# Linear attention followed by a mixture of adapters: where the gating steps stand in a hand-written order, how the last three outputs are grouped, and which queue stores the last one

## The chip, the cores and the metric

The kernel runs on one core of a Trainium2 chip. The metric is the device time of one execution in microseconds (us). Three runs of the kernel before took 119.56, 119.78 and 119.87 us; the median is 119.78. The core has a matrix engine (TensorE, "PE" in the profile, its weight loads "PEld"), a vector engine (VectorE, "DVE"), a scalar engine (ScalarE, "ACT"), GpSimd ("POOL") and a queue that only issues transfers here (SyncE, "SP"). Each engine executes its own instructions in the order in which they were written; engines wait for each other through semaphores.

## The reference

Inputs q, k and v have the shape (8 batches, 8 heads, 576 positions, 64). First comes a linear attention with cosine and sine weights on the positions, then, on its output x (4608 rows of 512), a mixture of 8 adapters of rank 16, of which each row uses its best two:

```python
q_p, k_p = phi(q, cos, sin), phi(k, cos, sin)   # relu, times cos and times sin: 128 features
kv  = einsum('bhsf,bhsd->bhfd', k_p, v);  z = sum(k_p, axis=2)
x   = einsum('bhsf,bhfd->bhsd', q_p, kv) / (einsum('bhsf,bhf->bhs', q_p, z) + 1e-6)
logits = x @ w_gate                              # 8 experts, the top 2 of each row
w      = softmax over the two chosen logits
out    = x + sum over the two of  w[e] * (x @ A[e]) @ B[e]
```

With two chosen logits l1 and l2 the softmax is a sigmoid: the weight of a chosen expert is sigmoid(2*l - (l1 + l2)), and that is how the kernel computes it.

## The kernel before

The output is made in 36 tiles of 128 rows and 512 columns; one step of the main loop ("slot" n, from 0 to 35) makes one tile of x. The work on one tile n goes through these functions:

- `transp_q(n)`, PE, L192: 16 small matmuls turn q and multiply it by the cos and sin diagonals, into two buffers of the two-buffer PSUM pool `qd`. `evac_q`, ACT, L208: two copies with relu. `move_q` is both; slot n calls it for tile n+1.
- `numden(n)`, PE, L226 and L231: numerator and denominator of the attention for all 8 heads, into the single PSUM tile `nd`.
- `normalise(n)`, DVE, L238 and L240: reciprocal and product, giving the tile `xt`. As there is one `nd`, `numden(n+1)` can only start when `normalise(n)` is through, and `normalise(n+1)` needs `numden(n+1)`.
- `transp_x(n)`, PE, L248, and `evac_x(n)`, DVE, L254: x transposed through the PSUM tile `xz`, giving `xT`. `evac_x(n)` is called at the start of slot n+1.
- `logits(n)`, PE, L274: four matmuls of 144 columns give x times all adapters A and x times the gate, into the single PSUM tile `za`.
- The gating of a group of three tiles: `gate_a` on DVE (L283 to L291: top values, their sum, mask, argument), `gate_sig` on ACT (L300, the sigmoid, written into `za` as well), `gate_b` on DVE (L307 and L309: the weights `em` and the weighted `zg`; after it `za` is free for the next group).
- `transp_z`, PE, L322: `zg` transposed into the second half of `xz`. The next `evac_x` takes it along (896 instead of 512 columns); the tile's tail is then `zgT`. Such a slot is in the table `move_at`.
- `delta(n)`, PE, L338 and L339: the identity times x, plus `zgT` times B, into one of two PSUM tiles `cd`, or, in slots in which `cd` holds a kv sum, into a `qd` buffer. `evac_o`, ACT, L347: copy to `osb`. `store`, L357 and L360: one transfer of 256 KB (two of 128 KB for a tile that mixes two batches), issued by SP.

In between the loop makes the kv sums of the next batches: `kv` on PE (L176, four or five columns of eight matmuls per slot, in 14 of the slots), whose scaled k comes from POOL (L152), ACT (L147) and DVE (L149, L161). All q, k and v have buffers of their own, and POOL issues their loads (L58) far ahead.

The order is written out by hand: the calls inside `with tc.manual_schedule()` are each engine's order. Tables tell in which slot something happens: `kv_at`, `relu_at`, `pool_at`, `logits_at`, `gate_a_at`, `gate_b_at`, `move_at`. In the kernel before, tiles 0 to 32 form eleven groups (0 to 10) of three, then come a group of two (33, 34) and a group of one (35). In a slot n the order is: `evac_x(n-1)`, `normalise(n)`, `move_q(n+1)`, `gate_sig` of a group whose slot for `gate_b` this is, the kv work, the due deltas with their copies and stores, `transp_x(n)`, `transp_z`, `gate_b`, k scaling, then `logits` ahead of `numden(n+1)`, or behind it in a slot with a `gate_b`, and last `gate_a`. What is left after slot 35 (a delta of group 9, all of group 10 but its gating, and the groups 11 and 12) follows behind the loop, the two last groups interleaved.

Of the kernel before, what the change touches and what calls it, by code (L numbers as in the profile page):

```python
# [8 lines left out]
FP32 = mybir.dt.float32  # L9
# [10 lines left out]
def kernel(ctx, tc, q, k, v, w_gate, A, Bw, out):  # L20
# [14 lines left out]
    p_kp = ctx.enter_context(tc.tile_pool(name="p_kp", bufs=3))  # L35
    p_qpt = ctx.enter_context(tc.tile_pool(name="p_qpt", bufs=6))
    p_kv = ctx.enter_context(tc.tile_pool(name="p_kv", bufs=3))
    p_x = ctx.enter_context(tc.tile_pool(name="p_x", bufs=12))
    p_xt = ctx.enter_context(tc.tile_pool(name="p_xt", bufs=6))
    p_g = ctx.enter_context(tc.tile_pool(name="p_g", bufs=3))  # L40
    p_o = ctx.enter_context(tc.tile_pool(name="p_o", bufs=8))
    qd = ctx.enter_context(tc.tile_pool(name="qd", bufs=2, space=bass.MemoryType.PSUM))
# [212 lines left out]
        if g is not None:  # L255
            zgT_t[g] = t[:, DCH:]

    groups = [list(range(i, min(i + 3, NT - 3))) for i in range(0, NT - 3, 3)]
    groups += [[NT - 3, NT - 2], [NT - 1]]
    group_of = {n: g for g, t in enumerate(groups) for n in t}  # L260

    def logits(n):
        g = group_of[n]
        i = n - groups[g][0]
        if i == 0:
            if g == len(groups) - 2:
                t = qd.tile([128, 512], FP32, name="zb", tag="qd")
            else:
                t = ps.tile([128, 512], FP32, name="za")
            za_t[g] = t[:, 0:3 * ZW].rearrange("p (i z) -> p i z", z=ZW)  # L270
            u_t[g] = t[:, 3 * ZW:3 * ZW + 3 * E].rearrange("p (i e) -> p i e", e=E)
        xT = xT_t.pop(n)
        for c in range(DCH):
            nc.tensor.matmul(out=za_t[g][:, i, :], lhsT=xT[:, c, :], rhs=AW[:, :, c, :],  # L274
                             start=(c == 0 and i == 0), stop=(c == DCH - 1),
                             skip_group_check=True)
# [19 lines left out]
    def gate_sig(g):  # L296
        n = len(groups[g])
        t, mask = g_t[g]
        u = u_t.pop(g)
        nc.scalar.activation(u[:, 0:n], t[:, 0:n], AF.Sigmoid)  # L300
        g_t[g] = (u, mask)
# [11 lines left out]

    def zT_ps(g):
        n = len(groups[g])
        at = 512 + (256 if g == len(groups) - 1 else 0)
        return xz[:, at:at + n * 128].rearrange("p (c s) -> p c s", c=n)

    def transp_z(g):
        zg = g_t.pop(g)  # L320
        for i in range(len(groups[g])):
            nc.tensor.transpose(out=zT_ps(g)[:, i], in_=zg[:, i], identity=ident)  # L322

    def evac_z(g):
        n = len(groups[g])
        zgT_t[g] = t = p_g.tile([128, 3, 128], BF16, name="zgT")
        nc.vector.tensor_copy(t[:, 0:n], zT_ps(g))

    dx_n = [0]

    def delta(n, own=True):
        g = group_of[n]
        if own:
            dx = cd[dx_n[0] % 2]
            dx_n[0] += 1
        else:
            dx = qd.tile([128, DM], FP32, name="dx", tag="qd")
        nc.tensor.matmul(out=dx, lhsT=ident, rhs=xt_t.pop(n), start=True, stop=False)  # L338
        nc.tensor.matmul(out=dx, lhsT=zgT_t[g][:, n - groups[g][0], :], rhs=Ball,  # L339
                         start=False, stop=True)  # L340
        osb_t[n] = dx

    def evac_o(n, eng="act"):
        src = osb_t[n]
        osb_t[n] = t = p_o.tile([128, DM], FP32, name="osb")
        if eng == "act":
            nc.scalar.copy(t, src)  # L347
        else:
            nc.vector.tensor_copy(t, src)

    def store(n):
        t = osb_t.pop(n)
        (b, s), (b1, s1) = tokens(n)
        if mixed(n):
            for rows_, b in ((lo, b), (hi, b1)):
                dst = out[b * S:(b + 1) * S, :].rearrange("(r s) d -> s r d", s=NS)[s]
                nc.sync.dma_start(out=dst, in_=t[rows_, :])  # L357
        else:
            dst = out[b * S:(b + 1) * S, :].rearrange("(r s) d -> r s d", s=NS)[:, s:s + 2, :]
            nc.sync.dma_start(out=dst, in_=t)  # L360


    kv_at, relu_at, pool_at, act_at, dve_at = {}, {}, {}, {}, {}
# [1 line left out]
    def put(at, step, what):  # L365
        at.setdefault(step, []).append(what)
# [18 lines left out]
                put(kv_at, first - ahead, (b, s))  # L385


    logits_at, gate_a_at, gate_b_at, move_at = {}, {}, {}, {}
    free = 5
    for g, t in enumerate(groups[:-2]):  # L390
        at = [max(n + 1, t[-1], free) for n in t]
        for n, a in zip(t, at):
            put(logits_at, a, n)
        free = at[-1] + (1 if g == len(groups) - 3 else 2)
        put(gate_a_at, free - 1, g)
        put(gate_b_at, free, g)
        put(move_at, free + 1, g)
    put(logits_at, NT - 2, NT - 3)

    def gate(g):  # L400
        gate_a(g)
        gate_sig(g)

    with tc.manual_schedule():
        for s in range(6):
            make_diag(s)
        wu = qd.tile([128, DM], FP32, name="wu", tag="qd")
        for i in range(24):
            nc.tensor.matmul(out=wu, lhsT=ones, rhs=wide, start=True, stop=True)  # L409
        for s in range(NS):  # L410
            scale_k(0, s, ("act" if s < 7 else "dve", "dve"))
            kv(0, s)
        nc.scalar.activation(warm, halfpi, AF.Sigmoid)
        for s in range(6, NS):
            make_diag(s)
        load_k(1)
        load_v(1)
        load_q(1)
        load_k(2)
        load_weights()  # L420
        load_v(2)
        load_q(2)
        load_k(3)
        load_v(3)
        load_k(4)
        load_q(3)
        load_v(4)
        kv_out(0)
        transp_q(0)
        evac_q(0, 0, "dve")  # L430
        evac_q(0, 1)
        numden(0)

        g10, g11, g12 = range(len(groups) - 3, len(groups))
        todo = []
        for n in range(NT):
            end = n == NT - 1
            if n > 0:
                g = move_at.get(n - 1, (None,))[0]
                evac_x(n - 1, g)  # L440
                if g is not None:
                    todo += groups[g]
            normalise(n)
            if not end and n != 3:
                move_q(n + 1)
            for g in gate_b_at.get(n, ()):
                gate_sig(g)
            for b, s in kv_at.get(n, ()):
                kv(b, s)
                if kv_n[b] == NS:  # L450
                    kv_out(b)
            if n == 3:
                move_q(n + 1)
            if end:
                transp_z(g10)
                logits(NT - 2)
            now = todo[:2 if len(todo) > 3 else 1]
            del todo[:len(now)]
            for d in now:
                delta(d, n not in kv_at)  # L460
                evac_o(d)
                store(d)
            transp_x(n)
            for g in move_at.get(n, ()):
                if not end:
                    transp_z(g)
            for g in gate_b_at.get(n, ()):
                gate_b(g)
            for b, s, i in dve_at.get(n, ()):
                scale_k1(b, s, i, "dve")  # L470
            for b, s0, s1 in relu_at.get(n, ()):
                relu_k(b, s0, s1)
            for b, s in pool_at.get(n, ()):
                scale_k(b, s)
                if s == 6:
                    if b + 3 < B:
                        load_k(b + 3)
                    if b + 2 < B:
                        load_q(b + 2)
                    if b + 3 < B:  # L480
                        load_v(b + 3)
            if n not in gate_b_at:
                for t in logits_at.get(n, ()):
                    logits(t)
            if n + 1 < NT:
                numden(n + 1)
            if n in gate_b_at:
                for t in logits_at.get(n, ()):
                    logits(t)
            for g in gate_a_at.get(n, ()):  # L490
                gate_a(g)
            for b, s, i in act_at.get(n, ()):
                scale_k1(b, s, i, "act")


        def finish(d, eng="act"):
            delta(d)
            evac_o(d, eng)
            store(d)

        evac_z(g10)
        evac_x(NT - 1)
        for d in todo + groups[g10][:1]:
            finish(d)
        logits(NT - 1)
        gate(g11)
        finish(NT - 5)
        gate(g12)
        gate_b(g11)
        transp_z(g11)  # L510
        finish(NT - 4)
        gate_b(g12)
        evac_z(g11)
        transp_z(g12)
        finish(NT - 3)
        evac_z(g12)
        finish(NT - 1, "dve")
        finish(NT - 2)

# [1 line left out]
_INS = ['q', 'k', 'v', 'moe_w_gate', 'moe_A', 'moe_B']  # L521
_OUTS = [((4608, 512), 'float32')]
# [25 lines left out]
```

## Time and profile before

| | |
|---|---|
| median of three runs | 119.78 us (119.56 to 119.87) |
| the profiled execution | 120.3 us, of it a span of 118.5 us from the first to the last instruction |
| mean granted TensorE clock | 0.997 |
| PE busy | 99.0 us, 84% of the span |
| DVE busy | 81.8 us, 69% |
| ACT busy | 76.8 us, 65% |
| POOL busy | 59.1 us, 50% |
| read from and written to memory | 28.85 MB and 9.44 MB |

Times in the views are counted from the start of the span, so the profiled execution's own time is 1.8 us more than its span. A matmul's end is modelled, and a busy PE is not a PE at its peak. The view of stretches gives, for one stretch of time, its length and each engine's busy time in it, then the granted clock, the share of the 16 DMA engines that was busy (values over 1 are a full set of engines) and GB/s. The view of waits gives who waited for whom, the sum, how often, and the longest. The chain that ended last is a list of start, length and what.

### The profile page before, as it was taken

To read this page: it belongs to the slowest core of one execution; us is meant where nothing else is said; L and a number is where in the kernel's file an instruction comes from. 1 tells how busy PE (TensorE), PEld (TensorE's weight loads), DVE (VectorE), ACT (ScalarE), POOL (GpSimd) and SP (SyncE) were. 2 spreads that over 40 slices of the span, in tenths; PEclk is the share of its full clock that TensorE was granted. 3 is DMA by queue.
4 is the path that set the end of the run, shared out by engine and by line. 5 is a ranking of instruction groups with operands and counts; after the bars stand their busy time and mean duration, and the time that the engine had idled before them with its cause. 6 is when DMAs were issued, how large, how long until landed. Compare 5 with 4: busy or idle time off the path is not lost.

```text
span 118.5 us, 4729 instructions
## 1 busy us (share of the span) xinstructions
PE 99.0 (84%) x1946; PEld 75.6 (64%) x1964; DVE 81.8 (69%) x293; ACT 76.8 (65%) x167; POOL 59.1 (50%) x118
## 2 busy tenths in 40 slices
PE   2997687868997999979999969989999999769720
PEld 1337567657885878758877857668787886656200
DVE  5697599389769765879667764797568637688620
ACT  5088579676357586688669835867779558574720
POOL 5982222278999994999990039719900000000000
PEclk9999999999999999999999999999999999999998
DMA  3999999999999999999999999999973333322892
GB/s 46 379 207 207 210 208 207 188 205 208 208 208 208 212 243 249 266 257 259 268 248 248 257 264 248 216 255 260 250 213 112 114 68 128 143 88 88 306 317 88
DMA packets 19654, 24.75 MB, mean 209 GB/s; under 512 B 2609, under 2 KB 14513, under 8 KB 19633
## 3 DMA queue, kind: packets, MB, share of 16 engines
q0 software_dynamic: 13856, 13.84, 69.9%
q1 hardware_dynamic: 5776, 10.62, 26.7%
q8 instruction: 15, 0.25, 0.8%
q14 instruction: 7, 0.05, 0.1%
HBM read 28.85 MB, written 9.44 MB: 323 GB/s over the span
## 4 chain that ended last, share of the span: by engine, by line
PE 36%; DMA 34%; DVE 9%; POOL 9%; ACT 4%; issue 4%; POOLq 0%; ACTq 0%
DMA q<-in_q_dram 23%; DMA v<-in_v_dram 12%; PE cd L176 8%; PE qd L192 7%; POOL kp L152 5%; PE xz L248 5%; PE za L274 5%; PE nd L231 4%; DVE xt L240 3%; PE cd L338 2%; DVE zg L309 2%; ACT qpT L208 2%; PE cd L339 2%; PE xz L322 1%; PE dx L338 1%
## 5 line engine op out<-in xcount | busy, mean ns | idle before, releaser
L208 ACT ACTIVATE qpT<-qd 128x512 bf16<-128x512 f32 x71 | 38.6, 595 | 23.5 <-PE qd L192 23.2
L254 DVE COPY xT<-xz 128x512 bf16<-128x512 bf16 (+1 forms) x36 | 17.1, 475 | 14.1 <-PE xz L322 8.8
L152 POOL TENSOR_SCALAR kp<-k,cos_tab 128x256 bf16<-128x256 bf16 x42 | 19.8, 471 | 13.1 <-DVE k L161 12.6
L240 DVE TENSOR_TENSOR xt<-nd,rden 128x512 bf16<-128x512 f32 x36 | 24.9, 692 | 1.2
L192 PE MATMUL qd<-diag,q 128*64 128x128 bf16 x576 | 23.0, 222 | 1.6 <-DMA q<-in_q_dram 1.6
L192 PEld LDWEIGHTS <-q 128*64 128x64 bf16 x576 | 17.2, 109 | 4.3 <-DMA q<-in_q_dram 2.0
L152 POOL TENSOR_SCALAR kp<-k,sin_tab 128x256 bf16<-128x256 bf16 x42 | 19.8, 470 | 0.0
L176 PE MATMUL cd<-v,kp 64*128 64x128 bf16 x576 | 19.0, 217 | 0.9 <-DMA v<-in_v_dram 0.7
L248 PEld LDWEIGHTS <-xt 128*128 128x128 bf16 x144 | 10.6, 115 | 12.5 <-DVE xt L240 8.3
L231 PE MATMUL nd<-kvsb,qpT 128*128 128x65 bf16 (+1 forms) x320 | 17.6, 195 | 0.9 <-DVE qpT L210 0.5
L176 PEld LDWEIGHTS <-kp 64*128 64x128 bf16 x576 | 16.3, 94 | 2.7 <-issue 1.0
L248 PE MATMUL xz<-ident,xt 128*128 128x128 bf16 x144 | 14.4, 223 | 4.1 <-DVE xt L240 3.5
L347 ACT COPY osb<-cd 128x512 f32<-128x512 f32 x24 | 14.1, 593 | 3.5 <-PE cd L339 3.4
L231 PEld LDWEIGHTS <-qpT 128*128 128x128 bf16 (+1 forms) x320 | 12.8, 99 | 2.1 <-DVE qpT L210 0.5
L274 PE MATMUL za<-AW,xT 128*128 128x144 bf16 x136 | 11.7, 225 | 2.1 <-DVE zg L309 2.1
L226 PE MATMUL nd<-eps_hi,ones 128*128 128x4 bf16 x72 | 11.6, 169 | 0.0
L274 PEld LDWEIGHTS <-xT 128*128 128x128 bf16 x144 | 9.7, 97 | 2.8 <-issue 2.4
L58 POOL DMA_DIRECT2D v<-in_v_dram x8 | 6.7, 839 | 5.1 <-DMA q<-in_q_dram 4.3
L238 DVE RECIPROCAL rden<-nd 128x8 f32<-128x8 f32 x36 | 7.3, 202 | 2.1 <-PE nd L231 2.0
L409 PE MATMUL wu<-wide,ones 128*128 128x512 bf16 x24 | 6.8, 449 | 2.2 <-DVE AW L111 2.2
L347 ACT COPY osb<-dx 128x512 f32<-128x512 f32 x11 | 6.4, 592 | 2.8 <-remote 2.8
L339 PE MATMUL cd<-Ball,xT 128*128 128x512 bf16 x18 | 6.8, 380 | 1.5 <-DVE xT L254 0.8
(66 smaller groups left out, 122.0 us busy)
## 6 DMA issues: line engine op xcount, KB each, us to landing
out_dram<-osb SPq DMA_DIRECT2D x32, 256.0 KB, 5.9
v<-in_v_dram POOLq DMA_DIRECT2D x8, 576.0 KB, 18.8
q<-in_q_dram POOLq DMA_DIRECT2D x8, 576.0 KB, 19.9
k<-in_k_dram POOLq DMA_DIRECT2D x7, 576.0 KB, 18.1
k0f<-in_k_dram SPq DMA_DIRECT2D x1, 1152.0 KB, 5.5
out_dram<-osb SPq DMA_DIRECT2D x8, 128.0 KB, 3.8
AW<-in_moe_A_dram POOLq DMA_DIRECT2D x1, 128.0 KB, 18.2
Ball<-in_moe_B_dram POOLq DMA_DIRECT2D x1, 128.0 KB, 16.5
```

Source lines behind the costliest of these rows:

```text
L152: nc.gpsimd.tensor_scalar(out=dst, in0=src, scalar1=tab, scalar2=1.0, op0=ALU.mult, op1=ALU.mult)
L176: nc.tensor.matmul(out=kvz[par][:, g], lhsT=kp_t[b][pr, s, g], rhs=v_rhs(b, g, s, pr), start=(first and g == 0), stop=(last and g == G - 1))
L192: nc.tensor.matmul(out=t[cols, j, 2 * gi:2 * gi + 2, :], lhsT=q_b[b][:, 2 * gp + gi, s, :], rhs=diag[:, s, i], start=(j == 0 and gi == 0), ...
L208: nc.scalar.activation(t, src, AF.Relu)
L226: nc.tensor.matmul(out=nd[:, gg, D:4 * W:W], lhsT=ones, rhs=eps_hi, start=True, stop=False, skip_group_check=True)
L231: nc.tensor.matmul(out=nd[pr, gg, j * W:(j + 1) * W], lhsT=qpT[:, j, pr], rhs=kv_t[b][:, h % 2, h // 2, :], start=False, stop=(j == 3), sk ...
L240: nc.vector.tensor_tensor(out=xt, in0=nd[:, :, :, 0:D], in1=rden.rearrange("p (g j) -> p g j", g=2).to_broadcast([128, 2, 4, D]), op=ALU.mult)
L248: nc.tensor.transpose(out=xz[:, c * 128:(c + 1) * 128], in_=x[:, c], identity=ident)
L254: nc.vector.tensor_copy(t[:, 0:c], xz[:, 0:c * 128].rearrange("p (c s) -> p c s", c=c))
L274: nc.tensor.matmul(out=za_t[g][:, i, :], lhsT=xT[:, c, :], rhs=AW[:, :, c, :], start=(c == 0 and i == 0), stop=(c == DCH - 1), skip_group_ ...
L339: nc.tensor.matmul(out=dx, lhsT=zgT_t[g][:, n - groups[g][0], :], rhs=Ball, start=False, stop=True)
L347: nc.scalar.copy(t, src)
```

## The change

Six things are changed.

1. The groups: twelve groups of three, so tiles 33, 34 and 35 are one group (11).
2. The tables for logits and gating. All logits of a group are now either `late` (behind `transp_x`, always ahead of `numden(n+1)`) or `early` (directly behind `transp_q`); up to group 7 all three tiles' logits stand in one slot, from group 8 on the third is `early` in the next one. `gate_a` stands in slot `at`, `gate_b` in `at + 1`, `move_at` is `at + 2`.
3. The order in a slot: `gate_a` and `gate_b` stand directly behind `normalise` on DVE, `gate_sig` stands in the slot of its `gate_a`, behind the copies of the deltas on ACT. `gate_b` so comes a slot after its sigmoid.
4. The loop ends at slot 34; slot 35 and what follows is written out. `zgT` of group 10 is copied by ACT, that of group 11 in two parts by DVE and ACT.
5. In the last group the products of x with the identity (`delta_x`) come ahead of the transposed `zg`, the products with B (`delta_z`) behind it; DVE copies the output of tile 34, ACT those of 33 and 35; the store of tile 35 is issued by ACT's queue.
6. The pool of `xt` has 14 buffers instead of 12, that of `xT` 7 instead of 6.

The slots that result, from 20 on (before | after):

```
slot  logits before    gate_a/gate_b/move   delta  | logits after         gate_a/gate_b/move   delta
20    18,19 (kv)       - / 5 / -            13     | -            (kv)    - / 5 / -            13
21    20    (kv)       - / - / 5            14     | 18,19,20     (kv)    - / - / 5            14
22    -                6 / - / -            15     | -                    6 / - / -            15
23    21,22            - / 6 / -            16     | -                    - / 6 / -            16
24    23               - / - / 6            17     | 21,22,23             - / - / 6            17
25    -     (kv)       7 / - / -            18     | -            (kv)    7 / - / -            18
26    24,25 (kv)       - / 7 / -            19     | 24,25        (kv)    - / 7 / -            19
27    26               - / - / 7            20     | 26 early             8 / - / 7            20
28    -                8 / - / -            21     | -                    - / 8 / -            21
29    27,28 (kv)       - / 8 / -            22     | 27,28        (kv)    - / - / 8            22
30    29    (kv)       - / - / 8            23     | 29 early     (kv)    9 / - / -            23,24
31    -                9 / - / -            24     | -                    - / 9 / -            25
32    30,31            - / 9 / -            25     | 30,31                - / - / 9            26
33    32               10 / - / 9           26     | 32 early             10 / - / -           27
34    33               - / 10 / -           27     | 33                   - / 10 / -           28
```

The core of the diff:

```diff
-    groups = [list(range(i, min(i + 3, NT - 3))) for i in range(0, NT - 3, 3)]
-    groups += [[NT - 3, NT - 2], [NT - 1]]
+    groups = [list(range(i, i + 3)) for i in range(0, NT, 3)]
...
-    def evac_z(g):
-        n = len(groups[g])
+    def evac_z(g, parts):
         zgT_t[g] = t = p_g.tile([128, 3, 128], BF16, name="zgT")
-        nc.vector.tensor_copy(t[:, 0:n], zT_ps(g))
+        for eng, i, j in parts:
+            if eng == "act":
+                nc.scalar.copy(t[:, i:j], zT_ps(g)[:, i:j])
+            else:
+                nc.vector.tensor_copy(t[:, i:j], zT_ps(g)[:, i:j])
...
-    free = 5
-    for g, t in enumerate(groups[:-2]):
-        at = [max(n + 1, t[-1], free) for n in t]
-        for n, a in zip(t, at):
-            put(logits_at, a, n)
-        free = at[-1] + (1 if g == len(groups) - 3 else 2)
-        put(gate_a_at, free - 1, g)
-        put(gate_b_at, free, g)
-        put(move_at, free + 1, g)
-    put(logits_at, NT - 2, NT - 3)
+    prev = 5
+    for g, t in enumerate(groups[:-1]):
+        tight = g > 7
+        at = max(t[-1] + (1 if tight else 2), prev + 1)
+        if g == 1:
+            at += 1
+        for n in t:
+            if n + 1 == at:
+                put(early_at, at, n)
+            else:
+                put(late_at, at - 1, n)
+        prev = at + 1
+        put(gate_a_at, at, g)
+        put(gate_b_at, at + 1, g)
+        put(move_at, at + 2, g)
+    put(late_at, NT - 2, NT - 3)
...
-    def delta(n, own=True):
+    def delta_x(n, own=True):
...
         nc.tensor.matmul(out=dx, lhsT=ident, rhs=xt_t.pop(n), start=True, stop=False)
+        osb_t[n] = dx
+    def delta_z(n):
+        g = group_of[n]
+        nc.tensor.matmul(out=osb_t[n], lhsT=zgT_t[g][:, n - groups[g][0], :], rhs=Ball,
                          start=False, stop=True)
...
             normalise(n)
-            if not end and n != 3:
+            if n != 3:
                 move_q(n + 1)
-            for g in gate_b_at.get(n, ()):
-                gate_sig(g)
+            for t in early_at.get(n, ()):
+                logits(t)
...
+            for g in gate_a_at.get(n, ()):
+                gate_a(g)
+            for g in gate_b_at.get(n, ()):
+                gate_b(g)
             now = todo[:2 if len(todo) > 3 else 1]
...
+                emit(d, n not in kv_at)
+            for g in gate_a_at.get(n, ()):
+                gate_sig(g)
             transp_x(n)
             for g in move_at.get(n, ()):
-                if not end:
-                    transp_z(g)
-            for g in gate_b_at.get(n, ()):
-                gate_b(g)
+                transp_z(g)
...
-            if n not in gate_b_at:
-                for t in logits_at.get(n, ()):
-                    logits(t)
-            if n + 1 < NT:
-                numden(n + 1)
-            if n in gate_b_at:
-                for t in logits_at.get(n, ()):
-                    logits(t)
-            for g in gate_a_at.get(n, ()):
-                gate_a(g)
+            for t in late_at.get(n, ()):
+                logits(t)
+            numden(n + 1)
...
+        evac_x(NT - 2)
+        normalise(NT - 1)
+        transp_z(last - 1)
+        logits(NT - 2)
+        evac_z(last - 1, [("act", 0, 3)])
+        todo += groups[last - 1]
+        for d in todo[:-3]:
+            emit(d)
+        transp_x(NT - 1)
+        emit(todo[-3])
+        evac_x(NT - 1)
+        logits(NT - 1)
+        emit(todo[-2])
+        gate_a(last)
+        gate_sig(last)
+        emit(todo[-1])
+        gate_b(last)
+        own = dict(zip(groups[last], (False, False, True)))
+        for d in groups[last]:
+            delta_x(d, own[d])
+        transp_z(last)
+        evac_z(last, [("dve", 0, 2), ("act", 2, 3)])
+        for d, e, q_eng in zip(groups[last], ("act", "dve", "act"),
+                               (nc.sync, nc.sync, nc.scalar)):
+            delta_z(d)
+            evac_o(d, e)
+            store(d, q_eng)
```

`emit(d)` is delta, `evac_o` and store of one tile; `delta_x` and `delta_z` are the two matmuls of `delta` apart.

## The prediction

> **What bounds the kernel now.** I read the chain that ended last first, then the waits of each engine, then stretches of the span one slot long. Below, X(n) is the time at which `transp_x(n)` starts on PE: the distance from X(n) to X(n+1) is one slot. The chain contains one long transfer and, directly behind it, PE. It is the load of q for batch 5, which `transp_q(22)` needs in slot 21.
>
> ```profile
> 43.02 26.73 DMA q<-in_q_dram
> ```
>
> The timeline of PE has the same place, with the wait in brackets:
>
> ```profile
> 69.79 0.53 PE L192 MATMUL qd<-diag,q 128*64 128x128 bf16 x12 [1.00 <-DMA q<-in_q_dram]
> ```
>
> So at 69.79 us PE had waited 1.00 us for a transfer that was under way for 26.73 us. Now the view of stretches; columns are the stretch, its length, then busy time of PE, PEld, DVE, ACT and POOL, the clock, the DMA share and GB/s. The first row is the part from slot 8 to that wait, the next ten are single slots, named by the X they start from (21, 23, 24, 26, 29, 30, 31, 32, 33 and 34), then X(21) to X(35) as a whole, the tail from X(35) to the end of the last copy, and two stretches at the very end.
>
> ```profile
> 34.30:69.50 35.20, 32.38 (x671) 25.92 (x673) 27.21 (x94) 25.00 (x56) 26.32 (x52) 1.00 1.17 245
> 71.91:74.36 2.45, 2.40 (x48) 1.70 (x47) 1.58 (x5) 1.51 (x5) 2.45 (x6) 1.00 1.17 254
> 76.17:79.33 3.16, 2.56 (x44) 2.00 (x44) 2.52 (x9) 2.10 (x6) 0.19 (x1) 1.00 1.17 245
> 79.33:82.21 2.88, 2.83 (x71) 2.41 (x70) 2.39 (x11) 2.40 (x5) 2.58 (x6) 1.00 1.15 273
> 85.42:87.75 2.33, 2.33 (x43) 1.90 (x43) 1.23 (x3) 1.45 (x4) 0.58 (x2) 1.00 0.96 250
> 92.51:95.87 3.36, 3.31 (x79) 2.83 (x80) 1.65 (x4) 2.01 (x5) 0.00 (x0) 1.00 0.43 99
> 95.87:98.32 2.45, 2.40 (x48) 1.70 (x47) 1.58 (x5) 1.51 (x5) 0.00 (x0) 1.00 0.16 59
> 98.32:100.13 1.81, 1.65 (x32) 1.20 (x33) 1.68 (x9) 1.49 (x4) 0.00 (x0) 1.00 0.18 66
> 100.13:103.13 3.00, 2.40 (x41) 1.84 (x41) 1.88 (x5) 1.54 (x4) 0.00 (x0) 1.00 0.47 174
> 103.13:106.14 3.01, 2.06 (x40) 1.65 (x39) 2.10 (x10) 2.53 (x7) 0.00 (x0) 1.00 0.26 92
> 106.14:107.99 1.85, 1.80 (x27) 1.34 (x28) 1.72 (x5) 0.23 (x1) 0.00 (x0) 1.00 0.22 81
> 71.91:107.99 36.08, 32.97 (x662) 25.83 (x670) 25.51 (x86) 24.76 (x55) 10.82 (x24) 1.00 0.69 172
> 107.99:114.16 6.17, 4.44 (x25) 1.82 (x25) 3.82 (x18) 4.27 (x9) 0.00 (x0) 1.00 0.70 232
> 114.00:116.00 2.00, 0.00 (x0) 0.00 (x0) 0.00 (x0) 0.16 (x1) 0.00 (x0) 1.00 1.03 382
> 116.00:118.00 2.00, 0.00 (x0) 0.00 (x0) 0.00 (x0) 0.00 (x0) 0.00 (x0) 0.94 0.11 42
> ```
>
> Three things are to be seen. Until slot 21 the DMA engines are full (share 1.17), so the load cannot come sooner by itself: 69.79 us is a pin. From X(21) at 71.91 to X(35) at 107.99 PE is busy for 32.97 of 36.08 us, and the 3.11 us of idle PE sit in few slots: 0.60 in slot 23 (76.17), 0.60 in slot 32 (100.13) and 0.95 in slot 33 (103.13), against 0.05 in slots with much PE work. In the tail PE idles 1.73 of 6.17 us. Who makes those slots wait:
>
> ```profile
> PEld L248 <- DVE xt L240: 8.3, 15, 0.7
> DVE em L307 <- ACT za L300: 5.8, 9, 0.7
> ```
>
> Nine times `gate_b` on DVE stands still for about 0.65 us, because its sigmoid stands behind two copies of q on ACT in the same slot; `evac_x` and the next `normalise` stand behind it on DVE, `logits` of the next group behind its release of `za` on PE.
>
> **The change part by part.** *Before the pin.* From slot 8 on to the pin PE gets one tile's logits more (3, 4, 5 move in from slot 7; 18, 19 move out to slot 21), about 0.25 us, and loses idle time, of which there is at most 35.20 - 32.38 = 2.82 us. PE arrives at `transp_q(22)` sooner by something between nothing and 2.6 us; I take 1.3 us, the middle. All of it turns into a longer wait for q. To be late there it would have to lose 1.00 us, while every removed wait works the other way. The stores of slots 9 to 20 share the engines with the loads; up to slot 20 both kernels store tiles 0 to 13, though tiles 3 to 8 come up to a slot later after. I leave the pin at 69.79; bounds one store's transfer each way, 256 KB at 382 GB/s = 0.69 us.
>
> *From X(21) to X(35).* The price list, from the chain at slot 27 where PE is never idle: delta 0.32 + 0.22, `transp_x` 0.22, `transp_z` 0.17, logits of one tile 0.25, `numden` 88.68 - 88.39 = 0.29, `transp_q` 0.57.
>
> ```profile
> 87.21 0.32 PE cd L338
> 87.53 0.22 PE cd L339
> 87.75 0.22 PE xz L248 x4
> 87.97 0.17 PE xz L322 x3
> 88.14 0.25 PE za L274 x4
> ...
> 88.68 0.57 PE qd L192 x16
> ```
>
> A slot without kv costs the larger of PE's sum and of the round from x to the next x. The round with a `gate_a` is the row 98.32 (1.81 us). The round with a `gate_b` that does not wait is slot 34 before:
>
> ```profile
> 106.00 0.17 DVE L307 TENSOR_TENSOR em<-za,mask 128x24 f32<-128x24 f32 x1
> 106.20 0.56 DVE L309 TENSOR_TENSOR zg<-za,em 128x384 bf16<-128x384 f32 x1
> ```
>
> There `em` starts without a wait, and the slot is 1.85 us long (row 106.14). Slot by slot, with nothing for the slots not named (22, 25, 27, 28: PE does the same and is the longer part, or the round is the same):
>
> - 21: two more tiles' logits, moved behind the pin: +0.50.
> - 23: the sigmoid wait and two tiles' logits go; 3.16 becomes 1.85: -1.31.
> - 24: two more logits in a slot that PE fills: +0.50. 26: one early: +0.25.
> - 29 (row 92.51): `transp_z` comes a slot sooner (0.17), tile 29's logits come early (0.25), and slot 30 has a second delta (two matmuls of 512 columns, 0.22 each where they follow each other): +0.86.
> - 30 (row 95.87): the same `transp_z` and logits are gone from this round: -0.42. 31 (row 98.32): a `gate_b` for a `gate_a`, 1.81 to 1.85: +0.04.
> - 32 (row 100.13): no wait for `zg`; PE's sum is 0.22 + 0.17 + 0.50 + 0.29 + 0.57 + 0.25 + 0.54 = 2.53 against 3.00: -0.47.
> - 33 (row 103.13): `gate_a` no longer waits for logits of the same stretch, no wide copy: 3.01 becomes 1.81: -1.20.
> - 34 (row 106.14): logits of 33 now wait for `zg`, which ends 0.6 behind X(34) (106.76); with 0.07 of hand-over, logits 0.25, `numden` 0.29 and, as an estimate, 1.0 to the next x (at most 1.3, the 1.81 of row 98.32 less `transp_x` and `numden`) it is 2.23 against 1.85: +0.38. Delta 29 fits into it.
>
> Sum: +0.50 - 1.31 + 0.50 + 0.25 + 0.86 - 0.42 + 0.04 - 0.47 - 1.20 + 0.38 = -0.87 us. It leaves PE about 1.3 us idle, where 3.11 were, with two logits and one delta more done. Bounds: -2.2 (no idle PE left) to +0.9 (slots 23, 32 and 33 save half of their 2.98, and slot 34 takes its 1.3).
>
> *The tail.* Here PE is not the bound but the one chain of a group of three, in us behind X(35). `evac_x(35)` ends at 0.87, logits of 35 at 1.3, `gate_a` takes 0.72 (103.98 to 104.70):
>
> ```profile
> 103.98 0.33 DVE m L283 x3
> 104.33 0.16 DVE nm L285
> 104.49 0.09 DVE mask L288
> 104.58 0.12 DVE tg L291
> ```
>
> So its result is there at 2.1. The sigmoid (0.20) stands on ACT behind the copy of tile 31, which ends at 2.4, at 0.59 a copy; it ends at 2.6, `gate_b` (0.2 + 0.56) at 3.4, three transposes at 3.8, DVE's two thirds of `zgT` (0.28) at 4.1.
>
> ```profile
> L347 ACT COPY osb<-cd 128x512 f32<-128x512 f32 x24 | 14.1, 593 | 3.5 <-PE cd L339 3.4
> ...
> L300 ACT ACTIVATE za<-tg 128x24 f32<-128x24 f32 x11 | 2.2, 202 | 0.0
> ```
>
> ACT's third follows; a short PSUM copy on ACT has no row, so it lies between nothing and 0.59; I take 0.3, nearer to DVE's 0.28 for twice the size. The identity products of tiles 33 to 35 are done in PE's idle time before. The copies then end at 5.2 (33, ACT), 5.5 (34, DVE 0.69) and 5.8 (35, ACT), where the last copy before ended at 6.17. Now the stores. Before, SP issued the last four 0.64 us apart, and its wait for the last ended 1.8 us after that:
>
> ```profile
> 112.24 2.56 SPq L360 DMA_DIRECT2D out_dram<-osb  x4
> ```
> ```profile
> SPq L543 <- DMA out_dram<-osb: 1.8, 1, 1.8
> ```
>
> 112.24 + 2.56 + 1.8 = 116.6: the last store landed 2.4 us after its copy ended (114.16), 8.6 behind X(35). After, the stores of 34 (SP, behind that of 33) and 35 (ACT) are both issued at 5.8. Alone, each would land at 8.2; sharing full engines (382 GB/s in the row 114.00), the second lands 0.69 later, at 8.9. I take 8.9, +0.3 against before, since that row shows the engines already full with stores of SP alone; bounds 8.2 (-0.4) and 9.5, with one more ACT copy of 0.59 ahead. ACT issuing a transfer has no row; nothing stands behind it on ACT.
>
> The Trainium skill, "Trainium Kernel Development and Optimization", section "Key Constraints", says that transfers from the SP, ACT and POOL queues use the same 16 engines and interleave, so that a second issuing engine saves issue time only. By that rule the last part of the change is worth only SP's issue and the tail is the 8.9 taken; by the trace, which has no store from ACT, 8.2 stays possible and the forecast would be 0.7 us lower.
>
> *Nothing elsewhere.* Two more `xt` and one more `xT` buffer remove no wait that the view shows; work is otherwise the same in number, and twelve groups instead of thirteen save DVE one set of small gating instructions, off the path. The sum is -0.87 + 0.3 = -0.57 us. The profiled execution took 120.3 us, so 119.7 on its own scale; it lies 0.5 above the median of 119.78, against which the forecast is 119.2 us.
>
> **The rivals.** (1) *The pin moves later, slower.* PE reaches slot 20 sooner, and the stores of 12 and 13 go ahead of the last packets of q for batch 5: up to 2 x 0.69 = 1.4 us, so -0.57 + 1.4 gives 120.6. It decides once q lands 0.9 us later. For it: the engines are full up to there. Against: tiles 3 to 8 leave later, which gives it back in part. (2) *The pin moves earlier, more gain.* Those later stores let q through one store earlier, 0.69: 118.5. Against: slots 14 and 16 store two tiles and catch up. (3) *The end does not do what it says, no change.* The sigmoid, `zgT` of group 10 and a third of `zgT` of group 11 are put on ACT, in order with the copies; one copy more (0.59) ahead of the chain takes back all: 119.8. For it: ACT is busy 4.27 of the tail's 6.17 us. Against: three identity products and a second engine for copies run beside. (4) *The clock falls in the longer wait.* PE would wait 1.0 + 1.3 = 2.3 us for q, at most 3.6. In the two last rows PE does nothing from 114.00 on at the latest, and the clock is 1.00 to 116.00, then 0.94: 2 us of idleness cost nothing. If the wait went over the point where it falls, the next slot's PE work of about 2.4 us at half speed gives 121.6. The Trainium skill, "TensorE: Matmul & The Clock Gate", section "Why this matters for your kernels", warns of idle gaps over about 3 us; the trace agrees as far as that 0.94 tells.
>
> **How the numbers follow.** Forecast 0.46, at 119.2 (own range 118.6 to 119.9); (1) 0.18, (2) 0.14, (3) 0.17, (4) 0.03, something else 0.02. A change of 0.3%, 0.36 us, is about what a measurement tells from none: faster is below 119.42, slower above 120.14. Faster: 0.65 of the forecast, all of (2), a little of (3): 0.47. Slower: (1), (4), and small parts of the forecast and (3): 0.28. The rest, 0.25, is the same. The range takes in (2) and (1), 118.3 to 120.6; a little over each end is left out.
>
> **What would show it.** Right: PE's wait for q in slot 21 grows from 1.00 to about 2.3 us and still ends near 69.8; the waits of `em` for ACT vanish; idle PE between X(21) and X(35) falls from 3.1 to about 1.3 us, and X(35) comes at 107.1; the last two stores land together, 8.9 us behind it. Wrong: q landing away from 69.8 by more than 0.7, slots 21, 24 and 29 growing more than slots 23, 32 and 33 shrink, or the sigmoid of the last group later than 2.7 us behind X(35).

## The result and the profile after

The changed kernel takes 121.19 us (median of 20 runs, 119.56 to 121.92) against 119.80 before (20 runs, 119.56 to 120.81): it is slower, where 119.2 was forecast. The ratio of the times is 1.0059, with a 95% interval of 1.0033 to 1.0086; it leaves out three runs that lie more than 1.5% above the fastest of this kernel. The two medians are 1.2% apart.

The runs of the changed kernel fall into two kinds. Six lie between 119.56 and 119.93, with a median of 119.74 and a mean granted TensorE clock of 0.981 to 0.992; fourteen lie between 121.06 and 121.92, with a clock of 0.964 to 0.979. (Two of the expectations below say seven and 13; that was a miscount.) Nothing lies between. The profiled run, 121.35 us with a clock of 0.979, is of the second kind.

The place that the prediction calls the pin, in the timeline of PE of the changed kernel, with the wait in brackets:

```profile
69.96 0.79 PE L192 MATMUL qd<-diag,q 128*64 128x128 bf16 x12 [2.24 <-DMA q<-in_q_dram]
70.68 2.31 PE L176 MATMUL cd<-v,kp 64*128 64x128 bf16 x40
```

q for batch 5 lands at 69.96 (69.79 before), and PE has waited 2.24 us for it instead of 1.00. But the 12 matmuls behind the wait take 0.79 us instead of 0.53, and the 40 of kv take 2.31 instead of 1.29. The view of stretches shows why. First the 3.41 us that end just behind the wait, then the next 3.41; then the slots that the prediction named, 21, 23, 24, 26, 29, 30, 32, 33 and 34, by the X they start from; then X(21) to X(35), and the tail:

```profile
66.66:70.07 3.41, 1.11 (x23) 0.85 (x24) 2.23 (x7) 0.59 (x1) 0.62 (x2) 1.00 1.16 257
70.07:73.48 3.41, 3.41 (x53) 2.77 (x53) 0.00 (x0) 1.54 (x4) 3.41 (x8) 0.50 1.18 248
73.62:76.57 2.95, 2.74 (x54) 2.20 (x55) 1.58 (x5) 1.35 (x4) 2.19 (x5) 1.00 1.22 209
78.38:80.23 1.85, 1.69 (x32) 1.23 (x32) 1.78 (x6) 1.85 (x5) 0.00 (x0) 1.00 1.15 266
80.23:83.80 3.57, 3.52 (x79) 3.10 (x80) 2.98 (x13) 2.45 (x5) 2.69 (x6) 1.00 1.17 250
86.65:89.02 2.37, 2.37 (x44) 2.00 (x44) 1.54 (x6) 1.55 (x5) 0.83 (x2) 1.00 0.56 164
93.78:98.08 4.30, 4.25 (x88) 3.48 (x89) 2.21 (x9) 2.44 (x6) 0.00 (x0) 1.00 0.33 71
98.08:100.12 2.04, 1.99 (x42) 1.29 (x40) 1.39 (x4) 1.68 (x5) 0.00 (x0) 1.00 0.20 72
101.97:104.53 2.56, 2.56 (x47) 2.20 (x48) 1.74 (x6) 1.63 (x4) 0.00 (x0) 1.00 0.45 170
104.53:106.28 1.75, 1.59 (x33) 1.16 (x32) 1.68 (x9) 1.53 (x5) 0.00 (x0) 1.00 0.18 61
106.28:108.70 2.42, 1.98 (x28) 1.33 (x27) 1.82 (x5) 1.57 (x4) 0.00 (x0) 1.00 0.39 144
73.62:108.70 35.08, 33.35 (x671) 26.26 (x679) 25.73 (x86) 25.62 (x57) 8.55 (x19) 1.00 0.67 169
108.70:114.42 5.72, 3.89 (x22) 1.59 (x23) 2.84 (x11) 3.57 (x8) 0.00 (x0) 1.00 0.67 214
```

For 3.41 us, from 70.07 to 73.48, the granted clock is 0.50, and this begins when PE has just begun to work again. In the 3.41 us before, PE was busy for 1.11 us. X(21) comes at 73.62. At full clock it would come 2.12 us behind q's landing, as before (69.79 to 71.91): at 72.08. So the half clock costs 1.54 us, which is the distance between the two kinds of runs. Behind X(21) most goes as forecast, almost slot by slot: 35.08 us to X(35), where 35.21 was forecast and 36.08 measured before (0.36 of the difference lies in slot 25, for which nothing was forecast; more on it below).

The end, in the waits of the transfer queue and its timeline:

```profile
112.44 2.73 SPq L364 DMA_DIRECT2D out_dram<-osb  x3
```
```profile
SPq L549 <- DMA out_dram<-osb: 2.5, 1, 2.5
```

The last store lands at 112.44 + 2.73 + 2.5 = 117.7, 9.0 us behind X(35); 8.9 was forecast.

### The profile page after: what moved, and what is told of

The parts are those of the page before. It is cut to its first block, busy times and chain, and to the rows that moved or that the text cites. A ratio compares the mean times of both kernels' runs of the same rounds, so it can differ in the third digit from the quotient of the medians.

```text
span 119.6 us, 4721 instructions
## 1 busy us (share of the span) xinstructions
PE 99.8 (83%) x1944; PEld 76.2 (64%) x1964; DVE 81.0 (68%) x286; ACT 77.4 (65%) x168; POOL 58.7 (49%) x118
## 4 chain that ended last, share of the span: by engine, by line
DMA 34%; PE 31%; POOL 15%; DVE 8%; issue 4%; ACT 3%; POOLq 0%; ACTq 0%; DVEq 0%
DMA q<-in_q_dram 22%; DMA v<-in_v_dram 12%; POOL kp L152 11%; PE cd L176 8%; PE qd L192 5%; PE xz L248 5%; PE nd L231 4%; DVE xt L240 4%; PE za L270 4%; PE dx L335 2%; POOL k L58 2%; POOL q L58 1%; ACT qpT L208 1%; PE cd L340 1%; DVE xT L254 1%
## 5 line engine op out<-in xcount | busy, mean ns | idle before, releaser
L192 PE MATMUL qd<-diag,q 128*64 128x128 bf16 x576 | 23.6, 223 | 2.9 <-DMA q<-in_q_dram 2.9
L176 PE MATMUL cd<-v,kp 64*128 64x128 bf16 x576 | 19.9, 223 | 1.0 <-DMA v<-in_v_dram 0.8
L176 PEld LDWEIGHTS <-kp 64*128 64x128 bf16 x576 | 17.1, 97 | 3.0 <-issue 0.9
L231 PE MATMUL nd<-kvsb,qpT 128*128 128x65 bf16 (+1 forms) x320 | 17.0, 194 | 0.8 <-DVE qpT L210 0.5
L351 ACT COPY osb<-cd 128x512 f32<-128x512 f32 x22 | 13.0, 595 | 1.1 <-PE cd L340 1.1
L351 ACT COPY osb<-dx 128x512 f32<-128x512 f32 x13 | 7.5, 594 | 3.3 <-remote 3.0
L58 POOL DMA_DIRECT2D v<-in_v_dram x8 | 6.2, 780 | 5.2 <-DMA q<-in_q_dram 4.4
L184 ACT CAST kvsb<-cd 128x260 bf16<-128x260 f32 x16 | 5.2, 379 | 4.9 <-PE cd L176 4.9
```

The lines of the kernel that those rows point to most:

```text
L58: eng.dma_start(out=t, in_=rows(dram, b))
L176: nc.tensor.matmul(out=kvz[par][:, g], lhsT=kp_t[b][pr, s, g], rhs=v_rhs(b, g, s, pr), start=(first and g == 0), stop=(last and g == G - 1))
L192: nc.tensor.matmul(out=t[cols, j, 2 * gi:2 * gi + 2, :], lhsT=q_b[b][:, 2 * gp + gi, s, :], rhs=diag[:, s, i], start=(j == 0 and gi == 0), ...
L231: nc.tensor.matmul(out=nd[pr, gg, j * W:(j + 1) * W], lhsT=qpT[:, j, pr], rhs=kv_t[b][:, h % 2, h // 2, :], start=False, stop=(j == 3), sk ...
```

## The experiments

The theories are the ones of the expectations: by the *clock theory* the changed order makes the wait for q long enough for the granted clock to fall, and that alone makes the kernel slower; by the *order theory* the lost time lies in the new order or in q's landing, with the clock only beside it. The *pin* is the claim that q's landing is set by the load stream, so that what PE gains ahead of it is lost. Each ratio is against runs of the kernel before that were taken beside the experiment, with medians of 119.98 to 120.16 us; a time set against 121.19, or against the 119.75 of the runs without a fall of the clock, is therefore good to a few tenths only.

**PE kept busy in the wait.** Ahead of `move_q(22)` in slot 21 of the changed kernel, eight matmuls whose result nobody reads:

```diff
+            if n == 21:
+                fl = ps.tile([128, 512], FP32, name="za")
+                for i in range(8):
+                    nc.tensor.matmul(out=fl, lhsT=ones, rhs=wide, start=True, stop=True)
             if n != 3:
                 move_q(n + 1)
```

> The changed kernel with eight matmuls of 512 columns (ones times ones, into the free za tile, 8 x 0.22 = 1.7 us, no result used) ahead of transp_q(22) in slot 21, inside the 2.24 us in which PE waits for q. Clock theory: the granted clock falls because PE idles there; with PE busy the clock stays at 1.00 behind the wait, the 13 runs at 121.1 to 121.9 disappear and all lie where the other seven were, 119.6 to 119.9. Order theory (the 1.5 us come from the new order or from q landing later, the clock being a companion): the runs stay at about 121.2, or get up to 0.3 slower still.

All twelve runs lie between 119.63 and 120.01, median 119.82, ratio to before 0.998 (0.9965 to 0.9994). The timeline of PE:

```profile
67.25 1.89 PE L459 MATMUL za<-wide,ones 128*128 128x512 bf16 x8
69.07 0.30 PE L192 MATMUL qd<-diag,q 128*64 128x128 bf16 x4
70.11 0.53 PE L192 MATMUL qd<-diag,q 128*64 128x128 bf16 x12 [0.74 <-DMA q<-in_q_dram]
70.57 1.29 PE L176 MATMUL cd<-v,kp 64*128 64x128 bf16 x40
```

q lands no sooner (70.11), the order is the changed one, PE does 1.9 us of work more, and the kernel is 1.4 us faster: kv takes 1.29 us again. That rules the order theory out.

**Less filling.** The same with `range(3)`.

> As the run with eight filling matmuls, but only three (0.65 us): PE still waits about 1.6 us for q in slot 21, between the 1.0 us of the kernel before (no fall of the clock) and the 2.24 us of the changed one (a fall in 13 of 20 runs). If the clock falls by how much of a stretch of fixed length PE was idle, with the stretch lying differently in each run, a smaller share of runs than 13 in 20 is slow, at 121.2, the others at 119.8; if every idle time over 1 us has the same chance, as many as before; order theory: all at 121.2.

PE's wait was 1.58 us. Eleven of twelve runs lie between 119.66 and 119.90; one took 121.65, with a clock of 0.969. Against 14 of 20 at 2.24 us, none of 12 at 0.74 us, and none of the 66 runs of the kernel before whose clock is on record (0.986 or more), which waits about 1 us: how often the clock falls grows steeply with the wait between 1.6 and 2.2 us. In the profiled run, without a fall, PE was busy for 1.78 of the 3.41 us up to just behind the wait:

```profile
66.60:70.01 3.41, 1.78 (x24) 0.98 (x23) 2.22 (x7) 0.59 (x1) 0.51 (x2) 1.00 1.16 255
```

**The wait lengthened in the kernel before.** One more load ahead of q for batch 5 in POOL's queue:

```diff
+                        if b == 3:
+                            nc.gpsimd.dma_start(out=scratch, in_=rows(v, 0)[:, 0:2, :])
                         load_q(b + 2)
```

> The kernel before with one more load of 288 KB (bf16 side; half of v of batch 0, into a tile that nobody reads) ahead of q for batch 5 in POOL's queue, and nothing else: q lands 1.4 to 2.2 us later, and PE's wait grows from 1.0 to between 2.4 and 3.2 us. Pin: the time rises by that delay. Clock theory: in many runs the granted clock falls behind the wait and 1.5 us come on top, so two kinds of runs, about 121.6 and 123.1. Order theory: no fall, all at 121.6, since the order is the one of before.

Six runs between 122.11 and 123.95, median 123.31; ratio 1.0243 (1.0194 to 1.0291). The two shortest, 122.11 and 122.38, have a clock of 0.990 and 0.991, the other four, from 123.19, 0.976 to 0.983. In the profile, of the longer kind, q lands at 71.64, 1.85 us later than before, and PE waits 2.29 us for it. Then this:

```profile
69.43:72.84 3.41, 1.20 (x40) 1.11 (x42) 1.17 (x5) 0.80 (x2) 2.28 (x6) 1.00 1.18 247
72.84:76.25 3.41, 3.19 (x41) 2.49 (x36) 0.62 (x1) 1.53 (x4) 3.41 (x9) 0.50 1.18 236
```

Again 3.41 us at 0.50, behind 3.41 us in which PE was busy for 1.20. The old order with a longer wait has the same fall. The Trainium skill, "TensorE: Matmul & The Clock Gate", section "What's actually happening", describes this: a free-running window of 3413 ns, and half the rate after an idle one. The length and the rate agree with these rows (3.41 us, 0.50). Its "idle" does not have to be a whole window: here the clock fell after windows in which PE was still busy for a third (1.11 and 1.20 of 3.41 us), and a wait of 2.24 us was enough.

Where the windows lie in a run without a fall in slot 21 can be read too, since the clock also falls once PE is done. In the changed kernel's trace it falls at 70.07 and again at 117.86 us, after it came back at 73.48: 44.38 us, which is 13 times 3.414. In the twelve traces without a fall in slot 21 the record of the clock at 1.00 is one piece of 105.81, 109.23 or 112.64 us, which is 31, 32 or 33 times 3.413. So each run has a grid of windows of its own, and PE's busy time in one window tells the clock of the next. The two closest cases, both at the end of the span, are these: first the second profile of the kernel before (`b_again1` below), then the changed kernel.

```profile
111.23:114.64 3.41, 1.70 (x7) 0.40 (x5) 0.92 (x2) 1.66 (x3) 0.00 (x0) 1.00 0.96 303
114.64:118.03 3.39, 0.00 (x0) 0.00 (x0) 0.00 (x0) 0.00 (x0) 0.00 (x0) 0.50 0.34 126
```
```profile
111.03:114.44 3.41, 1.72 (x8) 0.48 (x7) 1.72 (x4) 2.10 (x6) 0.00 (x0) 1.00 0.78 234
114.44:117.86 3.42, 0.00 (x0) 0.00 (x0) 0.00 (x0) 0.00 (x0) 0.00 (x0) 1.00 0.62 230
```

After 1.70 us the clock fell, after 1.72 it did not. Over all 14 traces each of the 16 falls comes behind a window with 1.70 us or less, and no fall comes behind the 430 windows with 1.72 or more (as the profile models PE's ends), so the border is half of the window, 1.71 us. The run with three filling matmuls had 1.79 us in its own window, 66.76 to 70.18. An estimate from this: laid at random over slot 21 of the changed kernel, a window gets less than 1.71 us in 0.67 of all positions (14 of 20 runs fell), over the late load's 0.69 (4 of 6), and in the profiles of the kernel before in none. This fits the position of the window deciding which runs fall; there is no profile of the changed kernel itself without a fall that would show it directly.

**Useful work in the wait.** In slot 21, kv ahead of `move_q(22)`:

```diff
-            if n != 3:
+            if n not in (3, 21):
                 move_q(n + 1)
...
-            if n == 3:
+            if n in (3, 21):
                 move_q(n + 1)
```

> The changed kernel with the five kv columns of slot 21 ahead of transp_q(22) instead of behind it: 1.22 us of useful PE work moves from behind the wait for q into it; the wait falls from 2.24 to about 1.0 us. Clock theory: no fall of the clock (before, a wait of 1.0 us had none) and 1.2 us less work behind the pin: 119.75 - 1.2 = 118.5. Order theory: only the 1.2 us, 121.2 - 1.2 = 120.0. If q's landing were not a pin (the wait just moves), no gain over 119.75.

119.10 us (119.05 to 119.21, six runs), ratio 0.9926 (0.991 to 0.9943). No run is of the longer kind, but 0.65 us gained over 119.75, not 1.2. The timeline of PE shows the rest:

```profile
69.88 0.53 PE L192 MATMUL qd<-diag,q 128*64 128x128 bf16 x12 [0.27 <-DMA q<-in_q_dram]
70.94 0.38 PE L335 MATMUL dx<-xt,ident 128*128 128x512 bf16 x1 [0.53 <-ACT qpT L208]
```

The delta of this slot uses a buffer of `qd`, and that is free only when ACT has copied q out; with kv behind `transp_q` this had been covered. A new wait of 0.53 us takes the place of a part of the old one.

The same edit in the kernel before:

> The kernel before with the same five kv columns ahead of transp_q(22). Its wait for q was 1.00 us, so all of it is filled: if q's landing at 69.8 is a pin, 1.0 us less, 118.8. If it is no pin (what is behind moves along with what is ahead), no change, 119.8. The clock theory expects no fall of the clock here either.

119.83 us (119.43 to 120.32, twelve runs), ratio 0.9993 (0.9973 to 1.0012): no change, a miss. Its timeline has no wait for q any more, but this:

```profile
70.02 0.64 PE L192 MATMUL qd<-diag,q 128*64 128x128 bf16 x16
71.33 0.38 PE L338 MATMUL dx<-xt,ident 128*128 128x512 bf16 x1 [0.67 <-ACT qpT L208]
```

kv, 1.29 us, is a little longer than the wait that it fills, and the delta then waits 0.67 us for ACT.

The late logits moved ahead as well:

```diff
+            if n == 21:
+                for t in late_at.pop(n):
+                    logits(t)
             if n in (3, 21):
                 move_q(n + 1)
```

> As the run with kv first, and the twelve matmuls of the logits of tiles 18 to 20 (0.75 us) ahead of transp_q(22) too; the wait for q falls to about 0.3 us. Behind transp_q(22), numden(22) then waits for the two ACT copies of q with less PE work in between, which I put at 0.2 to 0.4 us. Clock theory: 118.5 - 0.75 + 0.3 = 118.0. Order theory: 119.5.

119.15 us (118.99 to 119.38, six runs), ratio 0.9931 (0.9912 to 0.9949): nothing beyond the edit before, where 118.0 was expected. And `transp_q(22)` behind kv, delta, `transp_x` and `transp_z`, ahead of the late logits:

> The changed kernel with transp_q(22) behind kv, delta, transp_x and transp_z of slot 21, ahead of the late logits, which cover the ACT copies of q. With kv alone moved, the delta then waited 0.53 us for a qd buffer that ACT's copy of q frees; here it comes first. PE's wait for q falls to about 0.2 us and X(22) should come about 1.2 us ahead of the run with kv moved: 119.1 - 1.2 = 117.9. If numden(22) waits for ACT longer than the 0.75 us of logits cover, 118.5; if something behind slot 22 is late for another load, 119.0.

119.33 us (119.07 to 119.98, eleven runs), ratio 0.9948 (0.9928 to 0.9969), not 117.9 but near the last case of the expectation, 119.0. X(22) did come 1.4 us sooner than with kv alone moved (72.92 against 74.31). The gain is gone at the next load:

```profile
82.14 0.64 PE L192 MATMUL qd<-diag,q 128*64 128x128 bf16 x16 [1.16 <-DMA q<-in_q_dram]
```

That is q for batch 6, a second pin. Of the other kernels only the one with the late logits moved waits there, 0.91 us.

**The pin itself moved.** q for batches 5 and 6 loaded ahead of k for 6 and 7, and the work on that k put later:

```diff
+                    if b + 2 < B and b > 2:
+                        load_q(b + 2)
                     if b + 3 < B:
                         load_k(b + 3)
-                    if b + 2 < B:
+                    if b + 2 < B and b <= 2:
                         load_q(b + 2)
...
-        at = {2: 5, 3: 8, 4: 12, 5: 15, 6: 21, 7: 24}[b]
+        at = {2: 5, 3: 8, 4: 12, 5: 15, 6: 22, 7: 26}[b]
```

> The changed kernel with q for batches 5, 6 (and the later ones) loaded ahead of k for batches 6 and 7 in POOL's queue, and relu and scaling of k of these two batches one and two slots later (22 and 26 instead of 21 and 24). Pin theory: q for batch 5 lands one load (4 us) sooner, about 66, ahead of transp_q(22), so PE does not wait in slot 21, the clock does not fall, and the order's gain ahead of the pin counts: 119.75 - 2.2 = 117.6, or 118.5 where k of batch 6 or 7, now later, holds DVE up. If something else than the order of the loads sets the place where PE waits, the time stays at 119.1 or more.

118.45 us (118.40 to 118.50, four runs), ratio 0.9857 (0.984 to 0.9875). The timeline of PE in slot 21 is without a gap:

```profile
67.49 0.64 PE L192 MATMUL qd<-diag,q 128*64 128x128 bf16 x16
68.06 1.29 PE L176 MATMUL cd<-v,kp 64*128 64x128 bf16 x40
```

The place where PE waits is set by the order of the loads, and 118.45 is the expectation's case in which k, now later, holds DVE up. What is left is a wait of 0.97 us at `transp_x(23)`, behind relu and scaling of k on DVE in slot 22. With them back in slot 21 (`6: 21, 7: 26`):

> The run with q loaded ahead of k, but relu and scaling of k of batch 6 back in slot 21. In slot 22 they held DVE up and PE waited 0.97 us for normalise(23); slot 21 has kv work on PE that covers DVE. k of batch 6 lands about 70, DVE would wait about 1 us for it there, beside PE's work. If so, 118.45 - 0.97 = 117.5. If k lands later than about 71, DVE's wait reaches PE and the time stays at 118.5 or rises.

117.57 us (117.47 to 117.74, five runs), ratio 0.98 (0.9772 to 0.9828): the best of all kernels here, 2% under the kernel before and 3% under the median of the changed one. The kernel before with its loads in this order was not run, so how much of the 2% the order of the loads would give without the change stays open.

**The last store.** In the kernel with kv moved, SP issues the last store again:

```diff
-                               (nc.sync, nc.sync, nc.scalar)):
+                               (nc.sync, nc.sync, nc.sync)):
```

> The run with kv moved, its last store issued by SP again instead of ACT (compared with that run, 119.05 to 119.21). The three last stores are issued within 0.6 us of each other; if the shared engines set the end, SP's issue of the last one 0.6 us later changes little: 0 to +0.2. If the issue sets it, +0.6: 119.7.

119.20 us (118.72 to 120.69, twelve runs) against 119.10 (119.05 to 119.21): no difference that can be told. Two of the twelve, 120.46 and 120.69, have a clock of 0.976 and 0.973; no profile shows whether it fell in slot 21 there (the profiled run, 118.72 us, waits 0.88 us for q and has no fall). In the timeline the last four stores follow each other on SP:

```profile
109.84 3.39 SPq L364 DMA_DIRECT2D out_dram<-osb  x4
```

From X(35) to the end of the span it is 10.84 us, against 10.86 with ACT's queue, so that queue is worth nothing that these runs show. The Trainium skill, "Trainium Kernel Development and Optimization", section "Key Constraints", says that a second issuing engine saves issue time only; nothing in these runs speaks against it (119.10 and 119.20 us).

**The kernel before, twice more**, for its profile.

> The kernel before once more, for its profile. The forecast took its gain off the median, while the profiled execution before was 0.5 us above it. If the 0.5 us are when q lands, a faster execution shows PE's wait for q in slot 21 shorter than 1.0 us (about 0.5 or less) and the part behind X(21) as long as before, 36.1 + 10.5 us.

> As the run before it: the kernel before, another execution's profile. The part from X(21) to the end stays within 0.2 us of 46.6; what differs from the first profile lies ahead of X(21).

They took 119.81 and 120.22 us. In the first, X(21) comes at 71.75, nearly as in the profile that the prediction used (71.91), with a wait for q of 0.64 us; in the second at 72.11, with 1.11 us. What differs is behind X(21). In the first of them:

```profile
71.75:107.50 35.75, 33.79 (x671) 25.80 (x670) 25.54 (x86) 24.75 (x55) 11.23 (x25) 1.00 0.71 174
82.05:84.90 2.85, 2.85 (x73) 2.38 (x72) 1.71 (x5) 2.10 (x6) 2.85 (x7) 1.00 1.17 240
```

Slot 25 takes 2.85 us, where it took 3.21 in the profile of the prediction; in the second of them it is 2.95. From X(21) to the end it is 46.3 us in both, against 46.6. So both expectations missed: of the 0.49 us between the first profile and the shorter of these, 0.16 lie ahead of X(21) and 0.33 behind it, nearly all in a stop in slot 25 that comes and goes. In it the 40 kv matmuls take 1.65 us instead of 1.29, with no wait that the view names; its cause is open. In the five profiles of the old order slot 25 takes 2.85 to 3.21 us, 3.03 on average; with the new order it takes 2.85 in all seven in which nothing waits for q for batch 6.

## Why the prediction was wrong

**The pin: right.** PE's wait was forecast to grow from 1.0 to 2.3 us; it grew to 2.24, and q landed at 69.96. Loading q sooner moved the wait away.

**The step that failed: rival 4, the clock in the longer wait, was given a chance of 0.03.** Its mechanism, its place and its sign were right, and it decided 14 of 20 runs. The reason given against it was that 2 us of idle PE at the end of the span did not lower the clock. That reading was wrong: what counts is for how much of a window of 3.41 us PE was busy, and the end of the span showed one position of that window, not the time that is safe. In that profile the windows lie like this:

```profile
110.93:114.34 3.41, 2.27 (x10) 0.79 (x11) 1.48 (x5) 1.75 (x3) 0.00 (x0) 1.00 0.95 303
114.34:117.75 3.41, 0.00 (x0) 0.00 (x0) 0.00 (x0) 0.00 (x0) 0.00 (x0) 1.00 0.57 210
117.75:118.52 0.77, 0.00 (x0) 0.00 (x0) 0.00 (x0) 0.00 (x0) 0.00 (x0) 0.50 0.04 11
```

PE ended in a window that it had already filled by two thirds, so the clock stayed at 1.00 through the whole next one and fell only at 117.75. The price of the fall was put at 2.4 us and is 1.54, since the fall ends after 3.41 us. That 121.6, the rival's time, lies near the measured 121.19 is partly luck: the price was 0.9 us too high and the 119.2 below it 0.5 too low.

**From X(21) to X(35): right.** Two rows of the prediction end late: it took X(24) and X(27) from the chain, 79.33 and 87.75, while `transp_x` starts at 79.17 and 87.58 in the timeline before:

```profile
79.17 0.39 PE L248 MATMUL xz<-ident,xt 128*128 128x128 bf16 x4
87.58 0.39 PE L248 MATMUL xz<-ident,xt 128*128 128x128 bf16 x4
```

So slot 23 was 3.00 us long and not 3.16, and only 1.15 of the forecast 1.31 could be had. (The terms of slot 32 add up to 2.54, not 2.53.) With the starts of the timeline, slot by slot (forecast, measured change to the first profile): 21 +0.50, +0.50; 23 -1.31, -1.15; 24 +0.50, +0.53; 26 +0.25, +0.21; 29 +0.86, +0.94; 30 -0.42, -0.42; 31 +0.04, +0.04; 32 -0.47, -0.44; 33 -1.20, -1.26; 34 +0.38, +0.57. These sum to -0.87 and -0.48. Of the slots for which nothing was forecast, 28 is 0.15 and 27 is 0.01 shorter, which makes -0.64. Slot 25 is 0.36 shorter in this comparison and about 0.2 against the average of the old order; nothing was forecast for it, so that part of the agreement is luck. PE's idle time fell from 3.11 to 1.73 us and not to 1.3, and `em` waits for ACT in none of these slots any more.

**The tail: right.** +0.3 was forecast; from X(35) to the end of the span it is 10.88 us against 10.53, +0.35.

**The sum without the clock: too good by 0.4 us.** Where the clock does not fall in slot 21, the changed kernel takes 119.56 to 119.93, median 119.74, and 119.82 with the eight filling matmuls, a gain of 0.0 to 0.2 us in place of 0.57. The parts, as averages of three profiles each (the three of the kernel before; the changed kernel and the two with filling): X(21) to X(35) went from 35.88 to 35.08, -0.80; the tail +0.35; and X(21), without the half clock, from 71.92 to 72.14, +0.22, because q lands later by as much (69.79, 69.63 and 69.99 before; 69.96, 70.11 and 69.99 after). That is -0.23. So even the forecast's own mechanism ends in "no change", above all by the pin, for which bounds had been given and nothing taken. Whether the change moves the pin is not shown: q's landing differs by 0.4 us between executions of one kernel, and in the run with kv moved and the last store on SP it is 69.54.

**Rivals 1 to 3.** If the pin moved later (1), it was by 0.2 and not 1.4; the 0.7 by which (2) would have moved it earlier was not seen. A sigmoid or copy late on ACT in the tail (3) was not seen; the chain there ran as in the sum.

## What to carry to other kernels

Time gained ahead of a transfer that is itself at the limit is not gained but turned into a wait, and a longer wait of the matrix engine can cost more than it seems: here 1.2 us more of waiting brought 3.41 us at half the clock, which cost 1.54 us. So first find what pins the stage (an operand that lands late although its queue is always full), move that or fill the wait with work that does not need it, and only then tune the order. A single wait without a fall of the clock is no proof that the next, somewhat longer one is free: look at whether a stretch of 3.41 us around it, wherever it begins, can have the engine busy for less than half, and at whether the runs of a kernel fall into two kinds.

## What was not expected of the hardware

The granted clock fell to 0.50 for 3.41 us when PE had already begun to work again, after a window of 3.41 us in which it was still busy for 1.1 to 1.2 us. The windows lie on a grid that differs from run to run, and in all 14 traces the clock fell behind every window with 1.70 us of PE or less, and behind none with 1.72 or more. At waits of 0.74, 1.58 and 2.24 us the runs with a fall were 0 of 12, 1 of 12 and 14 of 20.
